# Loads of x gated, the first batch re-ordered, squares in pairs and second-layer work moved forward in a fused attention and feed-forward kernel

## Chip, cores and metric

The kernel runs on one core of one Trainium2 chip. The metric is the device time of one execution in microseconds (us). Executions of one kernel differ in time and in the clock that TensorE is granted, so several were taken of each. An execution more than 1.5% above the fastest of its kernel is labelled slow; on one core that is all a label can say.

TensorE is called PE, its weight load PEld, VectorE DVE, ScalarE ACT and GpSimd POOL. SP issues DMAs, and so does POOL. PSUM is the memory in which the kernel collects PE's sums. A transpose or load "lands" when its data is there.

## The reference, cut to what matters

```python
# x: 8 x 8 x 512 x 64, state: 8 x 8 x 32 x 64 (batch, head, tokens, depth), float32
scores = scale * x @ state.T ;  a  = softmax(scores)  ;  xread = a @ state
scores2 = scale * state @ x.T;  a2 = softmax(scores2) ;  sread = a2 @ x
X = concat([xread, sread], tokens)      # 544 tokens per batch, 512 features
r = maximum(X @ w_in, 0)                # w_in: 512 x 2048
out = (s * (r * r) + b) @ w_out         # w_out: 2048 x 512
```

## The kernel before

For each batch the kernel transposes x (`xT`), makes the scores `T`, their exponentials `E`, the sums `D`, the logarithm `L`, the reciprocal `R` and the weights `a`. It never forms `xread`: since `xread @ w_in` is `a @ (state @ w_in)`, it makes `M = state @ w_in` in four quarters and then `h = a @ M` in 16 tiles of 128 features. A tile is closed by a relu (`r`), a square (`g`) and later used by the second layer (`o`):

```python
    def mm1_close(key, hps, ntok, f):
        gt = gpool.tile([P, ntok], FP16, name=f"g_{key}_{f}", tag="g")
        r16 = rpool.tile([P, ntok], FP16, name=f"r_{key}_{f}", tag="r")
        if key == 0 and f % 4 == 1:
            nc.vector.tensor_scalar(r16, hps, 0.0, None, ALU.max)
        else:
            nc.scalar.activation(r16, hps, AF.Relu)
        nc.vector.tensor_mul(gt, r16, r16)
        G[key, f] = gt
```

The order of PE, SP and POOL is fixed by hand (`manual_schedule`). A "unit" is four second-layer matmuls; one follows each first-layer tile, and units lag about one batch behind. The batch `s` also prepares batch `s+1`:

```python
        for s in range(1, B):
            todo_s = pieces(s)
            for f in range(NKF):          # 16 tiles
                mm1_x(s, f)
                for fn in todo_s.get(f, []):
                    fn()
                if s == 1 and f == 4:
                    continue
                unit(todo.pop(0))
```

The loads of weights and of x, which also cast to 16 bits, go through one queue that POOL feeds: four quarters of `w_in` (wi), x1, `w_out` (wo), the state, x2 and then, at once, x3 to x7. From batch 2 on, `xT` is made by a DMA transpose that SP issues, as is `ET` (the transposed exponentials):

```python
            if s == 1:
                at(0, lambda: att_xT_dma(2))
                at(0, lambda: att_ET(0))
                at(0, lambda: att_ET(1))
                ...
                at(10, lambda: att_T(2, [0, 1]))
                at(11, lambda: att_ET(2))
                at(11, lambda: att_xT_dma(3))
```

Batch 0 is the opening: its x comes in float32 and is cast on DVE and ACT, and its transposes run on PE. A few idle matmuls (`warm_up`) keep PE active meanwhile.

The softmax here doesn't subtract the row's maximum and nothing guards it: scores larger than these inputs give would overflow.

## Time and profile before

| | before |
|---|---|
| median time (first runs) | 236.88 us (236.38 to 238.37, 3 runs) |
| profiled span | 235.9 us |
| PE busy | 220.0 us, 93% |
| first h of batch 1 starts | 32.46 us |
| PE ends | 232.6 us |

The profiled execution is not one of the three timed ones; it took 238.07 us at a mean granted clock of 0.971, among the slower of this kernel.

First, lines of the page of the kernel before: the busy time of PE, then the span in 40 slices of 5.9 us, where a digit is the busy share in tenths and 9 means 90% or more; PEclk is the granted clock in tenths of full speed.

```profile
...
PE 220.0 (93%) x1623; PEld 98.0 (42%) x1623; DVE 120.5 (51%) x269; ACT 122.4 (52%) x213; POOL 36.0 (15%) x67
...
PE   5989689989849999999999999999999999999994
...
PEclk9659999999988999999999999999999999999999
...
```

From about the fourteenth slice on PE is full, at full clock. What a change of order can win lies before 72 us. The next view lists what PE waited for: total us, how often, longest.

```profile
...
engine line waited for: us in total, times, longest us
PE T L64 <- DMA xT<-xn: 5.0, 2, 3.8
PE stTps L64 <- DVE st L461: 1.5, 1, 1.5
...
```

The largest is T, the scores of batches 2 and 3, waiting for the DMA transpose of x. The chain of waits of the kernel before, cut to 75 us, shows start, length, and what the time went to:

```profile
...
1.18 4.15 DMA stf<-in_state_dram
...
13.16 1.87 PE h L64 x4
...
19.13 0.68 DVE r L305
...
20.41 1.01 DVE g L308 x3
...
34.55 16.46 DMA xT<-xn
...
56.94 10.98 DMA xT<-xn
...
68.70 1.45 PE o L64 x4
...
```

The chain begins with the load of the state tile, runs through casts to the first h at 13.16, is mostly on DVE from 18.8 to 26.2 us, and then sits twice on a transpose: one issued at 34.55 that took 16.46 us to land, and one that took 10.98. The lines of SP in the timeline show why the second starts late: its issues stand in a fixed order, and the transpose of x3 stands behind the slow first one and three ET.

```profile
...
34.55 7.28 SPq L180 DMA_TRANSPOSE xT<-xn  x1
41.93 14.84 SPq L259 DMA_TRANSPOSE ET<-E  x3
56.94 5.61 SPq L180 DMA_TRANSPOSE xT<-xn  x1
```

Last, the busy time of each engine in chosen stretches of the kernel before (us, then per engine busy us and count; then granted clock, DMA share, GB/s):

```profile
...
core 0: us, PE busy (x) PEld busy (x) DVE busy (x) ACT busy (x) POOL busy (x), PEclk, DMA share, GB/s
4.20:7.60 3.40, 1.70 (x14) 0.67 (x12) 2.05 (x7) 1.15 (x3) 3.40 (x6) 1.00 1.19 285
7.60:17.85 10.25, 8.94 (x55) 3.05 (x56) 5.20 (x14) 6.46 (x15) 3.18 (x4) 0.50 1.30 204
20.00:25.00 5.00, 4.20 (x35) 2.00 (x34) 4.94 (x15) 2.84 (x6) 0.00 (x0) 1.00 1.24 206
65.60:69.00 3.40, 0.95 (x26) 0.51 (x27) 0.26 (x1) 0.42 (x1) 0.00 (x0) 1.00 0.52 151
69.00:72.40 3.40, 3.40 (x10) 1.18 (x8) 1.47 (x3) 1.44 (x5) 0.00 (x0) 0.51 0.00 0
...
```

Two stretches run at half clock, 7.6 to 17.85 and 69.0 to 72.4 us. Each follows a stretch of 3.4 us in which PE was busy half the time or less. The Trainium skill, "TensorE: Matmul & The Clock Gate", Part 1, puts PE at half rate after an idle window of about 3.4 us. From 20 to 25 us DVE is full.

### The profile page before, as it was taken

The page shows a single profiled execution, that of the slowest core. Times are in us where ns is not written, and L with a number is a line of the kernel's source. Part 1 is how long each engine was busy: PE and PEld are TensorE (multiplying, and loading weights), DVE is VectorE, ACT ScalarE, POOL GpSimd, SP SyncE. Part 2 cuts the span into 40 slices and gives each one's busy share as a digit, 9 for nine tenths or more (in the row PEclk, how much of TensorE's full clock was granted, in tenths as well). Part 3 has the DMA queues.
Part 4 walks back from the last instruction along what each step waited for, and adds up shares of the span by engine and source line. Part 5 has one row for each costly group of instructions (what it writes and reads, how often), then busy time and mean ns, then how long its engine had stood idle before and what let it go on. Part 6 is the DMA issues. An engine that isn't in the chain of part 4 may idle for free.

```text
span 235.9 us, 4108 instructions
## 1 busy us (share of the span) xinstructions
PE 220.0 (93%) x1623; PEld 98.0 (42%) x1623; DVE 120.5 (51%) x269; ACT 122.4 (52%) x213; POOL 36.0 (15%) x67
## 2 busy tenths in 40 slices
PE   5989689989849999999999999999999999999994
PEld 1323233334313444434443444344444444465653
DVE  1559844844523655474547454745474544533421
ACT  3566845358526634874487448744874444323300
POOL 8530053100100000000000000000000011000033
PEclk9659999999988999999999999999999999999999
DMA  6999999999930162621165116211311111111113
GB/s 192 210 202 207 202 126 136 146 183 221 169 121 0 47 152 74 148 74 47 44 148 78 44 49 150 74 47 44 89 47 44 44 47 46 65 72 44 44 44 89
DMA packets 38774, 23.68 MB, mean 100 GB/s; under 512 B 24100, under 2 KB 36644, under 8 KB 38756
## 3 DMA queue, kind: packets, MB, share of 16 engines
q0 software_dynamic: 15792, 16.72, 34.6%
q1 hardware_dynamic: 22548, 6.62, 17.6%
q8 instruction: 12, 0.20, 0.4%
q10 hardware_dynamic: 416, 0.10, 0.2%
q14 instruction: 6, 0.05, 0.1%
HBM read 17.33 MB, written 8.91 MB: 111 GB/s over the span
## 4 chain that ended last, share of the span: by engine, by line
PE 79%; DMA 13%; DVE 4%; ACT 2%; issue 1%; ACTq 0%
PE o L64 44%; PE h L64 20%; DMA xT<-xn 12%; PE Mps L64 3%; PE h_sr L64 3%; PE o_sr L64 3%; DMA stf<-in_state_dram 2%; PE D L64 2%; PE T L64 1%; PE V L64 1%; DVE g L308 1%; DVE M L249 1%; DVE xT L173 1%; PE xTps L64 1%; ACT r L307 1%
## 5 line engine op out<-in xcount | busy, mean ns | idle before, releaser
L64 PE MATMUL o<-wo,g 128*128 128x512 f16 (+1 forms) x528 | 132.4, 376 | 0.7 <-ACT M L250 0.7
L307 ACT ACTIVATE r<-h 128x512 f16<-128x512 f32 x124 | 73.5, 597 | 73.5 <-PE h L64 73.4
L308 DVE TENSOR_TENSOR g<-r 128x512 f16<-128x512 f16 x128 | 53.7, 423 | 63.0 <-ACT r L307 61.9
L64 PE MATMUL h<-a,M 128*128 128x512 f16 x256 | 77.6, 390 | 2.8 <-DVE M L249 1.4
L64 PEld LDWEIGHTS <-g 128*128 128x128 f16 x528 | 49.0, 98 | 55.5 <-issue 8.9
L350 POOL DMA_DIRECT2D out_dram<-osb x31 | 16.9, 544 | 166.9 <-DVE osb L348 128.0
L64 PEld LDWEIGHTS <-M 128*128 128x128 f16 x256 | 25.1, 100 | 35.0 <-issue 6.3
L348 DVE SCALAR_TENSOR_TENSOR osb<-o,s_bc,bias_bc 128x512 f32<-128x512 f32 (+1 forms) x33 | 24.1, 730 | 4.1 <-PE o L64 4.0
L254 DVE CAST M<-Mps 128x1024 f16<-128x1024 f32 x13 | 15.9, 1220 | 4.7 <-PE Mps L64 4.6
L64 PE MATMUL Mps<-wi,stT 64*32 64x512 f16 x256 | 13.5, 397 | 0.7 <-ACT r L307 0.4
L252 ACT CAST M<-Mps 128x1024 f16<-128x1024 f32 x13 | 13.1, 1008 | 0.0
L64 PEld LDWEIGHTS <-stT 64*32 64x32 f16 x384 | 4.7, 90 | 19.4 <-issue 15.4
L203 ACT ACTIVATE E<-T 128x512 f16<-128x512 f32 x16 | 9.4, 596 | 6.4 <-PE T L64 6.4
L307 ACT ACTIVATE r_sr<-h_sr 128x256 f16<-128x256 f32 x16 | 6.1, 384 | 11.4 <-PE h_sr L64 11.3
L228 DVE TENSOR_TENSOR a<-E,R 128x1024 f16<-128x1024 f16 (+1 forms) x9 | 5.7, 632 | 10.0 <-ACT R L227 10.0
L308 DVE TENSOR_TENSOR g_sr<-r_sr 128x256 f16<-128x256 f16 x16 | 4.7, 292 | 10.1 <-ACT r_sr L307 9.5
L64 PE MATMUL h_sr<-srdT,wi 128*128 128x256 f16 x64 | 9.3, 272 | 0.1
L64 PE MATMUL T<-xT,stT 64*32 64x256 f16 x128 | 4.0, 288 | 5.0 <-DMA xT<-xn 5.0
L227 ACT ACTIVATE R<-L 128x1024 f16<-128x1024 f32 (+1 forms) x9 | 8.5, 959 | 0.2
L226 ACT ACTIVATE L<-D 128x1024 f32<-128x1024 f32 (+1 forms) x9 | 8.3, 924 | 0.2 <-PE D L64 0.2
L64 PEld LDWEIGHTS <-wi 128*128 128x128 f16 x64 | 6.2, 97 | 3.7 <-issue 0.4
L64 PE MATMUL o_sr<-wo,g_sr 128*128 128x512 f16 x32 | 7.1, 379 | 0.0
(53 smaller groups left out, 90.1 us busy)
## 6 DMA issues: line engine op xcount, KB each, us to landing
out_dram<-osb POOLq DMA_DIRECT2D x31, 256.0 KB, 2.5
xn<-in_x_dram POOLq DMA_DIRECT2D x7, 512.0 KB, 15.3
wi<-in_moe_w_in_dram POOLq DMA_DIRECT2D x4, 512.0 KB, 10.5
wo<-in_moe_w_out_dram POOLq DMA_DIRECT2D x4, 512.0 KB, 19.7
xf<-in_x_dram SPq DMA_DIRECT2D x2, 512.0 KB, 5.0
out_dram<-osb_sr POOLq DMA_DIRECT2D x8, 64.0 KB, 1.9
out_dram<-osb SPq DMA_DIRECT2D x2, 128.0 KB
st<-in_state_dram POOLq DMA_DIRECT2D x1, 192.0 KB, 19.6
```

What stands on the lines that cost most here:

```text
L64: return nc.tensor.matmul(out, lhsT, rhs, start=start, stop=stop, tile_position=tp, is_transpose=is_transpose, skip_group_check=True,)
L173: eng(dst[:, h2 * i : h2 * i + h2], two[i].rearrange("p (q t) -> p q t", q=h2),)
L203: nc.scalar.activation(a["E"][:, g, :].rearrange("p (m t) -> p m t", m=2), T[:, :, 256 * i : 256 * i + 256], AF.Exp, scale=scale, accum_ou ...
L226: nc.scalar.activation(a["L"][:, sl], Dps, AF.Ln)
L227: nc.scalar.activation(a["R"][:, sl], a["L"][:, sl], AF.Exp, scale=-1.0)
L228: nc.vector.tensor_mul(a["a4"][:, sl], a["E"][:, sl], a["R"][:, sl])
L252: nc.scalar.copy(dst, ps)
L254: nc.vector.tensor_copy(dst, ps)
L307: nc.scalar.activation(r16, hps, AF.Relu)
L308: nc.vector.tensor_mul(gt, r16, r16)
L348: nc.vector.scalar_tensor_tensor(osb, ops, s_bc, bias_bc[:, n0:n1], ALU.mult, ALU.add)
L350: eng.dma_start(dst, osb[p0:p1])
```

## The change

Its intent: keep x loads away from the transposes that PE needs next; shorten the chain of the opening; save DVE time by squaring two tiles at once; and give PE second-layer work inside batch 0, where it has gaps. The diff is cut to its core; some smaller moves are left out (the PSUM pool of some h tiles, and the places of the bias sum and of two M copies in batch 1):

```diff
     def mm1_close(key, hps, ntok, f):
+        if f % 2 == 0:
+            R2[key] = rpool.tile([P, 2, ntok], FP16, ...)
+        r16 = R2[key]
+        if key == 0 and f in (1, 5):                 # was f % 4 == 1
+            nc.vector.tensor_scalar(r16[:, f % 2], hps, 0.0, None, ALU.max)
         ...
+        if f % 2 == 1:
+            nc.vector.tensor_mul(gt, r16, r16)       # 128 x 2 x ntok
@@ issue order on POOL
         load_wi(0)
         load_wi(1)
+        cast_st(nc.gpsimd, 0, 1)
         load_wi(2)
+        cast_x0(1, 1, nc.gpsimd.tensor_copy)
+        cast_st(nc.gpsimd, 1, 2)
         load_x(1)
         load_wi(3)
         ...
-        for b in range(3, B):
-            load_x(b)
@@ batch 0, start
-        warm_up(8); cast_st; att_stT(0); cast_x0 x4; att_xT_pe(0, 0); warm_up(2)
-        att_xT_pe(0, 1); att_T(0, [0]); warm_up(1); att_T(0, [1]); att_D(0, [0])
-        cast_st; att_stT(1); att_D(0, [1]); att_M(0, 0)
+        warm_up(11); cast_x0 x2; att_xT_pe(0, 0); att_stT(0); cast_x0; warm_up(2)
+        att_T(0, [0]); att_xT_pe(0, 1); att_D(0, [0]); warm_up(1); att_T(0, [1])
+        att_stT(1); att_M(0, 0); att_D(0, [1]); warm_up(2)
@@ batch 0, rest
-            7: [att_M(1, 0, "split")], 9: [broadcast_sb, att_xT_pe(1, 0)],
-            10: [att_xT_pe(1, 1)], 11: [att_M(0, 3, "split"), att_T(1)],
-            13: [att_D(1)], 14: [att_M(1, 1, "split")]
+            7: [att_xT_pe(1, 0)], 8: [broadcast_sb], 9: [att_xT_pe(1, 1)],
+            10: [att_M(0, 3, "dve"), att_T(1)], 11: [att_D(1)],
+            12: [att_M(1, 0, "act"), unit(units[0])], 13: [unit(units[1])],
+            14: [att_M(1, 1, "dve"), unit(units[2])], 15: [unit(units[3])]
-        for i in range(2): unit(units[i])            # two units after batch 0
@@ batches 1 and later
+            nc.gpsimd.tensor_copy(gate, A[2]["xT"][0:1, 0, 0, 0:1])   # POOL waits for xT of x2
+            load_x(3)
-                at(11, lambda: att_xT_dma(3))
+                at(8, lambda: att_xT_dma(3))
+                at(12, lambda: load_x(4))
+            if s + 3 < B: at(9, lambda: load_x(s + 3))
```

More of the change, by code (lines that the diff above doesn't have):

```diff
@@ L52 @@
     apool = ctx.enter_context(tc.tile_pool(name="apool", bufs=2))
-    gpool = ctx.enter_context(tc.tile_pool(name="gpool", bufs=3 * NKF))
+    gpool = ctx.enter_context(tc.tile_pool(name="gpool", bufs=3 * NKF // 2))
     rpool = ctx.enter_context(tc.tile_pool(name="rpool", bufs=4))
@@ L90 @@
     st16 = konst.tile([P, 2 * B, 2, D], FP16, name="st16")
+    gate = konst.tile([1, 1], FP16, name="gate")
     xf = konst.tile([P, NG, NQ, SCH * D], FP32, name="xf")
@@ L249, in att_M @@
             nc.vector.tensor_copy(dst[:, 0], two[0])
-            nc.scalar.copy(dst[:, 1], two[1])
+            (nc.vector.tensor_copy if b + c == 0 else nc.scalar.copy)(dst[:, 1], two[1])
         elif how == "act":
@@ L293 @@
     G = {}
+    R2 = {}
     def mm1_open(key, ntok, f):
@@ L297, in mm1_open @@
         if key == 0 and f % 2 == 1:
-            pool, tag = (psA, "att") if f < 8 else (psO, "o")
+            pool, tag = (psA, "att") if f < 8 else (psH, "h")
         return pool.tile([P, ntok], FP32, tag=tag, name=f"h_{key}_{f}")
     def mm1_close(key, hps, ntok, f):
-        gt = gpool.tile([P, ntok], FP16, name=f"g_{key}_{f}", tag="g")
-        r16 = rpool.tile([P, ntok], FP16, name=f"r_{key}_{f}", tag="r")
-        if key == 0 and f % 4 == 1:
-            nc.vector.tensor_scalar(r16, hps, 0.0, None, ALU.max)
-        else:
-            nc.scalar.activation(r16, hps, AF.Relu)
-        nc.vector.tensor_mul(gt, r16, r16)
-        G[key, f] = gt
+        if f % 2 == 0:
+            R2[key] = rpool.tile([P, 2, ntok], FP16, name=f"r_{key}_{f}", tag="r")
+        r16 = R2[key]
+        if key == 0 and f in (1, 5):
+            nc.vector.tensor_scalar(r16[:, f % 2], hps, 0.0, None, ALU.max)
+        else:
+            nc.scalar.activation(r16[:, f % 2], hps, AF.Relu)
+        if f % 2 == 1:
+            gt = gpool.tile([P, 2, ntok], FP16, name=f"g_{key}_{f}", tag="g")
+            nc.vector.tensor_mul(gt, r16, r16)
+            G[key, f - 1] = gt[:, 0]
+            G[key, f] = gt[:, 1]
     def mm1_k(b, f, g, hps):
@@ L459, in cast_st, with cast_x0 @@
         def cast_st(eng, b0, b1):
-            for k in range(2):
-                eng.tensor_copy(st16[:, 2 * b0 : 2 * b1, k, :], stf[:, 2 * b0 : 2 * b1])
+            n = 2 * (b1 - b0)
+            src = stf[:, 2 * b0 : 2 * b1].unsqueeze(2).broadcast_to([P, n, 2, D])
+            eng.tensor_copy(st16[:, 2 * b0 : 2 * b1], src)
+        def cast_x0(g, half, eng):
+            h2 = NQ // 2
+            src = xf[:, g, half * h2 : half * h2 + h2]
+            dst = xn[0].rearrange("p (q g) c d -> p g q (c d)", g=NG)[
+                :, g, half * h2 : half * h2 + h2
+            ]
+            eng(dst, src)
         load_wi(0)
         load_wi(1)
+        cast_st(nc.gpsimd, 0, 1)
         load_wi(2)
+        cast_x0(1, 1, nc.gpsimd.tensor_copy)
+        cast_st(nc.gpsimd, 1, 2)
         load_x(1)
@@ L472 @@
         nc.gpsimd.tensor_copy(st16[:, 4:, 1, :], st16[:, 4:, 0, :])
-        for b in range(3, B):
-            load_x(b)
-        def cast_x0(g, half, eng):
-            h2 = NQ // 2
-            src = xf[:, g, half * h2 : half * h2 + h2]
-            dst = xn[0].rearrange("p (q g) c d -> p g q (c d)", g=NG)[
-                :, g, half * h2 : half * h2 + h2
-            ]
-            eng(dst, src)
-        warm_up(8)
-        cast_st(nc.vector, 0, 1)
+        warm_up(11)
+        cast_x0(0, 0, nc.vector.tensor_copy)
+        cast_x0(0, 1, nc.scalar.copy)
+        att_xT_pe(0, 0)
         att_stT(0)
-        for g in range(NG):
-            cast_x0(g, 0, nc.vector.tensor_copy)
-            cast_x0(g, 1, nc.scalar.copy)
-        att_xT_pe(0, 0)
+        cast_x0(1, 0, nc.vector.tensor_copy)
         warm_up(2)
+        att_T(0, [0])
         att_xT_pe(0, 1)
-        att_T(0, [0])
+        att_D(0, [0])
         warm_up(1)
         att_T(0, [1])
-        att_D(0, [0])
-        cast_st(nc.vector, 1, 2)
         att_stT(1)
+        att_M(0, 0, "split")
         att_D(0, [1])
-        att_M(0, 0, "split")
+        warm_up(2)
         mm1_x4(0, 0, lambda: att_M(0, 1, "split"))
@@ L504 @@
             5: [lambda: att_M(0, 2, "split")],
-            7: [lambda: att_M(1, 0, "split")],
-            9: [broadcast_sb, lambda: att_xT_pe(1, 0)],
-            10: [lambda: att_xT_pe(1, 1)],
-            11: [lambda: att_M(0, 3, "split"), lambda: att_T(1, [0, 1])],
-            13: [lambda: att_D(1, [0, 1])],
-            14: [lambda: att_M(1, 1, "split")],
+            7: [lambda: att_xT_pe(1, 0)],
+            8: [broadcast_sb],
+            9: [lambda: att_xT_pe(1, 1)],
+            10: [lambda: att_M(0, 3, "dve"), lambda: att_T(1, [0, 1])],
+            11: [lambda: att_D(1, [0, 1])],
+            12: [lambda: att_M(1, 0, "act"), lambda: unit(units[0])],
+            13: [lambda: unit(units[1])],
+            14: [lambda: att_M(1, 1, "dve"), lambda: unit(units[2])],
+            15: [lambda: unit(units[3])],
         }
@@ L515, with gated_x3 @@
                 fn()
-        for i in range(2):
-            unit(units[i])
-        todo = units[2:]
+        todo = units[4:]
+        def gated_x3():
+            nc.gpsimd.tensor_copy(gate, A[2]["xT"][0:1, 0, 0, 0:1])
+            load_x(3)
         def pieces(s):
@@ L528, in pieces @@
                 at(0, lambda: att_xT_dma(2))
+                at(0, gated_x3)
                 at(0, lambda: att_ET(0))
                 at(0, lambda: att_ET(1))
-                at(1, lambda: att_M(1, 2, "dve"))
-                at(3, lambda: att_M(1, 3, "act"))
-                at(4, bias_sum)
-                at(5, bias_end)
+                at(8, lambda: att_xT_dma(3))
+                at(12, lambda: load_x(4))
+                at(3, lambda: att_M(1, 2, "dve"))
+                at(5, lambda: att_M(1, 3, "act"))
+                at(2, bias_sum)
+                at(3, bias_end)
                 at(6, lambda: att_stT(2))
@@ L544, in pieces @@
                 return out
+            if s + 3 < B:
+                at(9, lambda: load_x(s + 3))
             if nb < B:
@@ L570 @@
                     fn()
-                if s == 1 and f == 4:
+                if s == 1 and f == 2:
                     continue
```

## The prediction

> **What bounds the kernel now.** TensorE (PE). The page gives PE 220.0 of 235.9 us (93%), DVE 51%, ACT 52%. From 70 to 232.6 us the slices show PE without gaps. What can be won lies before 72 us:
>
> - Opening (0 to 32.5 us, where the first matmul of batch 1 starts). The chain of waits runs DMA of the state tile to 5.3, casts, transposes, exponentials, first h at 13.16; from 18.8 to 26.2 it sits on DVE (r, M casts, g, xT copies). DVE is busy 4.94 of the 5 us from 20. The granted clock is 0.50 from 7.6 to 17.85 us, after a stretch (4.2 to 7.6) in which PE was busy only 1.70 of 3.4 us.
> - Two waits for the DMA transposes of x: 1.14 us at 51 and 3.81 us at 68 (waits of PE). Those transposes took 16.5 and 11.0 us from issue to landing against 4.3 for the best one, because five x loads queued at 33 us share the engines. The 3.8 us gap also brings a half clock from 69.0 to 72.4, about 1.7 us more. The Trainium skill, "TensorE: Matmul & The Clock Gate", Part 1, gives half rate after one idle window of about 3.4 us; the trace agrees (0.5, in multiples of 3.41 us).
>
> **What the change does.**
>
> 1. Gating x3 behind xT2, spreading x4 to x7, and issuing xT3 three slots earlier. x2 lands near 34.4 as before; xT2 then runs nearly alone (landed near 40, needed near 45); xT3 lands near 52, needed near 59. Gain: 1.1 + 3.8 + 1.7 = 6.6 us, all on the critical path.
> 2. Opening order. The x0 cast no longer waits behind the state casts on DVE; E0 starts near 7.6 instead of 9.25, first h near 11.9 instead of 13.2, the second half of h near 13.2 instead of 15.5. Extra warm-ups (5 matmuls) fill otherwise idle PE and probably keep the clock. GpSimd casts delay the issue of later loads by about 3 us, but the software queue is serial at about 2.6 us per 0.5 MB tensor and has issues in hand: no later landings.
> 3. Squares in pairs: 128x512 took 423 ns, 128x1024 (a<-E,R) 692, so 154 ns per pair, about 1.2 us of DVE in batch 0; two relu's (0.69 us each) go from DVE to ACT. Later DVE is half idle: worth nothing.
> 4. Four second-layer units (0.86 us each) sit inside batch 0 in idle PE, against two after it. Batch 1 starts near 30.0 instead of 32.5 with 1.73 us more work done: opening gain about 4.2 us.
>
> **Prediction.** 236.9 - 6.6 - 4.2 + about 0.3 for clock risk: **226.3 us**, 8 in 10 within 223.5 to 229.5. Faster by over 2%: 0.95; within 2%: 0.04; slower: 0.01.
>
> **What would show it.** Waits of PE on DMA xT gone; granted clock 1.0 at 65 to 75; batch 1's first h near 30; first second-layer matmul near 25 instead of 30.7; g in 64 plus 8 pairs of about 0.69 us and 0.42 us.
>
> **What would make it wrong.** PE near 20 to 24 us waits for DVE, then ACT's exponentials: a window under half busy would bring a half clock there (1 to 2 us). The half clock at 7.6 may remain. GpSimd casts slower than 1 us would delay wi2, x1 and everything behind them, x2 and xT2 included. The GpSimd gate holds back the first outputs; if that reached the output buffers, DVE and then PE would stall.

## The result, and the profile after

| | before | after |
|---|---|---|
| median time | 237.41 us (236.38 to 238.37, 4 runs) | 225.44 us (225.28 to 225.51, 4 runs) |
| profiled span | 235.9 | 223.5 |
| PE busy | 220.0 (93%) | 215.9 (97%) |
| first h of batch 1 | 32.46 | 28.95, with two more units done |
| PE ends | 232.6 | 220.1 |

The ratio is 0.9495 (95% interval 0.945 to 0.9541). Ratios here are the mean time of one kernel's fast runs over that of the other's of the same rounds, so not quite the ratio of the medians quoted. PE starts the first h of batch 1 earlier, before and after:

```profile
...
32.46 0.59 PE L64 MATMUL h<-a,M 128*128 128x512 f16 x2
...
28.95 0.59 PE L64 MATMUL h<-a,M 128*128 128x512 f16 x2
...
```

The page of the changed kernel, the same lines (slices of 5.6 us):

```profile
...
PE 215.9 (97%) x1628; PEld 97.8 (44%) x1628; DVE 113.2 (51%) x191; ACT 121.9 (55%) x211; POOL 37.7 (17%) x71
...
PE   7887999999999999999999999999999999999993
...
PEclk9999999999999999999999999999999999999999
...
```

PE is at 90% or more from the fifth slice to the last but one, and the clock is never lowered. The waits of PE in the changed kernel:

```profile
...
PE warm_ps L64 <- DVE warm L447: 1.2, 1, 1.2
PE Mps L64 <- DMA wi<-in_moe_w_in_dram: 0.9, 1, 0.9
PE D L64 <- DVE M L255: 0.5, 1, 0.5
PE xTps L64 <- DMA xn<-in_x_dram: 0.5, 1, 0.5
...
```

No wait for a transpose is left; two small waits for loads (wi, x1) are new. SP's lines in the timeline:

```profile
...
34.55 1.98 SPq L181 DMA_TRANSPOSE xT<-xn  x1
36.64 3.06 SPq L260 DMA_TRANSPOSE ET<-E  x2
46.22 2.85 SPq L181 DMA_TRANSPOSE xT<-xn  x1
...
```

The transpose of x2 is issued at 34.55 as before, but occupies SP for 1.98 us instead of 7.28, and the one of x3 goes out at 46.22 instead of 56.94. The stretches, for comparison:

```profile
...
4.20:7.60 3.40, 3.22 (x25) 1.41 (x24) 1.70 (x4) 1.33 (x3) 1.93 (x4) 1.00 1.19 279
7.60:17.85 10.25, 8.96 (x74) 3.52 (x74) 8.02 (x16) 7.72 (x16) 6.68 (x9) 1.00 1.30 206
20.00:25.00 5.00, 3.99 (x44) 1.43 (x45) 2.85 (x6) 3.90 (x9) 0.00 (x0) 1.00 1.24 206
...
```

The bookkeeping of the profiled spans: 235.9 - 223.5 = 12.4 us. Up to the first h of batch 1 the gain is 32.46 - 28.95 = 3.5 us, and two units more are done by then (8 matmuls at 0.216 us, 1.7 us): 5.2 us. The other 7.2 us are the two waits (1.14 + 3.81), about 1.8 us of half clock behind the second (the four o matmuls at 68.70 took 1.45 us on the chain of waits and the next four 1.65, against 0.86 at full clock; the h between them 0.85 against 0.43), and 0.35 us before the bias matmul.

This compares a longer than usual execution of the kernel before (238.07 us, clock 0.971, half clock for 10.24 us of its opening) with an ordinary one of the changed kernel (225.28 us). Profiles of the same old opening in other runs reached the first h of batch 1 sooner: at 30.86 us with no half clock (fill_wait) and at 31.07 and 31.90 us with 3.4 us of it (gate_warm, which has three more idle matmuls, and gate_only). So about 1.6 of the 5.2 us go with the clock of that one execution.

### The profile page after: what moved, and what is told of

It is laid out like the page before. It is cut to its first block, busy times and chain, and to the rows that moved or that the text cites. A ratio compares the mean times of both kernels' runs of the same rounds, so it can differ in the third digit from the quotient of the medians.

```text
span 223.5 us, 3970 instructions
## 1 busy us (share of the span) xinstructions
PE 215.9 (97%) x1628; PEld 97.8 (44%) x1628; DVE 113.2 (51%) x191; ACT 121.9 (55%) x211; POOL 37.7 (17%) x71
## 4 chain that ended last, share of the span: by engine, by line
PE 89%; DMA 8%; DVE 1%; POOL 1%; SPq 0%; issue 0%
PE o L64 51%; PE h L64 22%; DMA wi<-in_moe_w_in_dram 5%; PE Mps L64 4%; PE h_sr L64 3%; PE o_sr L64 3%; DMA stf<-in_state_dram 2%; PE D L64 2%; PE V L64 1%; PE T L64 1%; DVE M L255 1%; PE bias_ps L64 0%; PE wsum_ps L64 0%; SPq L450 0%; POOL xn L106 0%; PE stTps L64 0%
## 5 line engine op out<-in xcount | busy, mean ns | idle before, releaser
L310 ACT ACTIVATE r<-h 128x512 f16<-128x512 f32 x126 | 74.3, 597 | 70.3 <-PE h L64 66.5
L64 PE MATMUL h<-a,M 128*128 128x512 f16 x256 | 75.5, 379 | 0.3 <-ACT r L310 0.3
L313 DVE TENSOR_TENSOR g<-r 128x1024 f16<-128x1024 f16 x64 | 44.1, 691 | 44.0 <-ACT r L310 43.6
L356 POOL DMA_DIRECT2D out_dram<-osb x31 | 16.9, 546 | 147.1 <-DVE osb L354 136.2
L64 PEld LDWEIGHTS <-M 128*128 128x128 f16 x256 | 24.6, 98 | 30.2 <-issue 1.7
L255 DVE CAST M<-Mps 128x1024 f16<-128x1024 f32 x15 | 18.3, 1223 | 2.5 <-PE Mps L64 2.2
L253 ACT CAST M<-Mps 128x1024 f16<-128x1024 f32 x14 | 14.1, 1008 | 0.0
L64 PE MATMUL Mps<-wi,stT 64*32 64x512 f16 x256 | 12.6, 383 | 1.0 <-DMA wi<-in_moe_w_in_dram 0.9
L64 PE MATMUL warm_ps<-warm 128*128 128x512 f16 x16 | 6.4, 549 | 1.3 <-DVE warm L447 1.2
L313 DVE TENSOR_TENSOR g_sr<-r_sr 128x512 f16<-128x512 f16 x8 | 3.4, 426 | 6.6 <-ACT r_sr L310 6.3
```

The source lines that it names most:

```text
L64: return nc.tensor.matmul(out, lhsT, rhs, start=start, stop=stop, tile_position=tp, is_transpose=is_transpose, skip_group_check=True,)
L253: nc.scalar.copy(dst, ps)
L255: nc.vector.tensor_copy(dst, ps)
L310: nc.scalar.activation(r16[:, f % 2], hps, AF.Relu)
L356: eng.dma_start(dst, osb[p0:p1])
```

## The experiments

Every experiment passed the check of its result. That includes no_load_wait, which computes the wrong thing, so on these inputs the check does not see that error. All were timed in five rounds against the kernel before. On those chips the kernel before took 237.13 to 237.79 us (medians of 11 runs). The changed kernel, repeated as a yardstick, took 225.65. It was repeated on one chip only, beside gate_only, no_gate and fill_wait; the other runs are compared with it across chips, on which the fast mean of the kernel before ranges from 236.2 to 237.4 us. Differences of under 1 us between such runs are soft.

**after_again: the changed kernel once more** (no edit).

> The changed kernel unchanged, as the yardstick on this chip. 225.3 to 225.6 us, ratio to before 0.945 to 0.954.

Measured: 225.65 us (225.32 to 227.02), ratio 0.9519 (0.9476 to 0.9563). The median is 0.05 above the range expected; the ratio is as expected. An effect below about 0.4 us is not told apart here.

### What the gate is worth

**gate_only: the gate without the rest.** In the kernel before:

```diff
-        for b in range(3, B): load_x(b)
+            gate copy, load_x(3) after xT of x2; load_x(4) at tile 12; load_x(s + 3) at tile 9
-                at(11, lambda: att_xT_dma(3))
+                at(8, lambda: att_xT_dma(3))
```

> The kernel before with only the gating of the x loads (x3 after the transpose of x2, x4 to x7 spread over the batches, transpose of x3 three slots earlier). My theory: the two waits of PE for the transposes (1.1 and 3.8 us) and the half clock after the second (1.7 us) go, so about 6.6 us faster than before, near 230.5 us; the opening keeps its 32.5 us and its half clock from 7.6 to 17.9. Rival A: the transposes are slow by themselves, or because of the stores and the other transposes, not because of the x loads: then the transpose of x3 still takes 10 us or more and the gain is under 3 us. Rival B: the gain needs the new opening as well: under 3 us.

Measured: 230.14 us (228.04 to 231.87), ratio 0.9667. On fast runs that is 7.5 us less than the kernel before (229.43 against 236.93); the medians differ by 7.4. PE's waits for transposes are gone from its profile. SP's lines:

```profile
...
34.60 1.98 SPq L181 DMA_TRANSPOSE xT<-xn  x1
...
46.99 6.35 SPq L181 DMA_TRANSPOSE xT<-xn  x1
...
```

Both rivals fall: the two transposes landed after 6.3 and 8.4 us instead of 16.5 and 11.0, and the gain needs no new opening. In this run the load of x4 (45.4 to 53.4 us) ran beside the second.

**no_gate: the rest without the gate.** In the changed kernel the loads of x3 to x7 go back behind x2, and the transpose of x3 to tile 11.

> The changed kernel with the loads of x put back as before (all five behind x2, transpose of x3 in its old place). My theory: the waits come back in full, since the new opening makes PE need the transposes earlier while x2 still lands at 34.4 us: 6.5 to 9 us slower than the changed kernel, 232 to 234 us, with PE waiting for the transposes of x2 and x3[...]. Rival (terms do not add): the opening and the gate share their gain, so that without the gate the opening's 5 us are lost again in the wait for x3, which is set by the DMA queue and not by PE: then near 236 us, equal to before within 1 us.

Measured: 235.77 us (234.21 to 238.98), ratio 0.9919 (0.9868 to 0.9969); on fast runs 9.5 us slower than the changed kernel and only 1.5 us faster than the kernel before. My range was 6.5 to 9, so the rival is nearer. Its PE waits hold this line:

```profile
...
PE T L64 <- DMA xT<-xn: 7.3, 2, 4.0
...
```

PE waited 7.3 us instead of 5.0. T of batch 3 starts at 66.74 us against 68.05 in the kernel before, though its first h of batch 1 started at 29.29 instead of 32.46: the transposes, not PE, set that time. So the terms do not add. The gate alone gives 7.5 us, the rest alone 1.5, both together 11.0 (236.93 - 225.92, same chip). Most of the opening's gain only counts once the gate has taken the transposes off the chain. The two waits also speak to the clock:

```profile
...
49.51 0.44 PE L64 MATMUL T<-xT,stT 64*32 64x256 f16 x16 [3.27 <-DMA xT<-xn]
49.88 1.04 PE L64 MATMUL o<-wo,g 128*128 128x512 f16 x4
...
66.74 0.65 PE L64 MATMUL T<-xT,stT 64*32 64x256 f16 x16 [4.05 <-DMA xT<-xn]
...
67.75 1.89 PE L64 MATMUL o<-wo,g 128*128 128x512 f16 x4
...
```

After a wait of 3.27 us four o matmuls took 1.04 us, full clock; after one of 4.05 us they took 1.89.

**fill_wait: does the half clock cost extra?** In the kernel before:

```diff
+                if s == 2:
+                    at(3, lambda: warm_up(9))
                 at(3, lambda: att_T(nb, [0, 1]))
```

> The kernel before with nine idle matmuls (1.9 us) put on PE inside its 3.8 us wait for the transpose of x3; they do nothing but keep PE active. My theory: the half clock from 69 to 72.4 us follows from the idle window and costs 1.7 us beyond the wait itself, so this kernel is 1.3 to 1.9 us faster than before though it does more work, and the clock stays at 1.0 at 65 to 75 us. Rival: the half clock costs nothing, or comes from something else: same time within 0.5 us.

Measured: 235.92 us (235.38 to 237.29), ratio 0.9955 (0.9905 to 1.0005). Medians differ by 1.65 us, fast means by 0.8, and the interval touches 1: the sign is likely, the size not settled. The profile shows why: the half clock after the second wait is gone, but in this execution the first wait, 2.0 us long, brought one. Its stretches:

```profile
...
48.40:51.81 3.41, 1.50 (x21) 0.69 (x22) 1.54 (x2) 1.17 (x4) 0.00 (x0) 0.96 1.35 183
51.81:55.22 3.41, 3.41 (x10) 1.19 (x9) 0.59 (x2) 0.95 (x4) 0.00 (x0) 0.54 1.36 184
...
```

PE was busy 1.50 of 3.41 us, and the next stretch ran at about half clock. (The trace's own clock record puts the change at 51.57 us; in the 3.42 us before it PE was busy for 1.42.)

A second reading of the clock needs no edit. The kernel before was executed 44 times beside the experiments, and 31 of these count as fast. Among the fast ones the eight with a mean granted clock of 0.99 or more took 235.9 us on average, the 17 between 0.98 and 0.99 took 237.0, and the six below 0.98 took 237.4. The changed kernel's ten executions all had 0.997 or more. So a part of the gain, of the order of 1 us, goes along with the clock; this is a correlation and not a test.

### What the opening is made of

**single_sq: one square per tile.** In the changed kernel:

```diff
-        if f % 2 == 1: nc.vector.tensor_mul(gt, r16, r16)
+        nc.vector.tensor_mul(gt[:, f % 2], r16[:, f % 2], r16[:, f % 2])
```

> The changed kernel with one square per tile of 128x512 again instead of one per pair. The prediction took 1.2 us of DVE time off a chain that it called DVE bound: then this is 1.0 to 1.4 us slower, near 226.8. My theory after seeing the trace: in the changed kernel PE waits in batch 0 for the loads of x1 and the last quarter of w_in (0.5 and 0.9 us), not for DVE, and a pair has to wait for both of its halves, so the pairing is worth nothing: within 0.4 us of 225.5.

Measured: 225.6 us (225.36 to 225.99), ratio 0.95. The pairing is worth nothing that can be seen. DVE was busy 7.74 of the 8 us from 13 to 21 us with single squares and 7.08 with pairs: 0.66 us saved, and spent waiting.

**fewer_warm: without the five added idle matmuls** (`warm_up(11)` to `warm_up(8)`, `warm_up(2)` ahead of the first h removed).

> The changed kernel without the five added idle matmuls (8 instead of 11 at the start, none ahead of the first h). Theory: they are what keeps the clock at 1.0 in the opening; without them a window with under half of it busy lets the clock fall to 0.5 between 7 and 18 us in most executions: 0.5 to 2 us slower, mean clock 0.98 to 0.995, larger spread. Rival: the new order alone keeps PE busy enough: within 0.3 us of 225.5, clock 1.0.

Measured: 225.5 us (225.29 to 225.67), mean clock 0.99 to 1.0. The rival holds: the added idle matmuls are worth nothing that can be seen.

**units_after: no units inside batch 0.**

```diff
-            12: [..., unit(units[0])], 13: [unit(units[1])], 14: [..., unit(units[2])], 15: [unit(units[3])]
+        for i in range(2): unit(units[i])      # after batch 0; todo = units[2:]
```

> The changed kernel with no second-layer unit inside batch 0; two follow it, as before the change. Theory: PE has no work to do while the exponentials of batch 1 are made (the first h of batch 1 can't start before 26.5 us), so of the 3.5 us of units about 1 us can't be hidden elsewhere: 0.7 to 1.5 us slower, near 226.6. Rival: batch 1 simply starts earlier by as much: within 0.3 us.

Measured: 227.58 us (227.11 to 229.08), ratio 0.9596; on fast means 2.0 to 2.5 us slower than the changed kernel. That is more than expected. In its PE timeline (start, us, operation, idle time before it) the gap is plain:

```profile
...
25.64 0.41 PE L64 MATMUL Mps<-wi,stT 64*32 64x512 f16 x8
27.46 0.59 PE L64 MATMUL h<-a,M 128*128 128x512 f16 x2 [1.42 <-ACT r L310]
...
```

The last h of batch 0 has to wait 1.42 us for the relu of an earlier tile to free its PSUM buffer, while ACT makes the reciprocal and copies M for batch 1 (1.06 and 1.01 us, from 24.95 on). In the changed kernel the units run there.

**casts_off_pool: casts on DVE and ACT, loads issued without a break.**

```diff
-        cast_st(nc.gpsimd, 0, 1) ... cast_x0(1, 1, nc.gpsimd.tensor_copy); cast_st(nc.gpsimd, 1, 2)
+        cast_st(nc.vector, 0, 1) ... cast_x0(1, 1, nc.scalar.copy); cast_st(nc.vector, 1, 2)
```

> The changed kernel with the casts of the state and of the last quarter of x0 on DVE and ACT instead of GpSimd, so that all loads are issued without a break. Theory: the loads land when the serial queue lets them, not when they are issued, so x1 and the last quarter of w_in land as before (16.7 and 19.3 us), and the exponentials start about 0.5 us later, which the waits for those loads swallow: 0 to 0.5 us slower. Rival A: the GpSimd casts delay the loads: 0.5 us or more faster, x1 landing earlier. Rival B: the cast chain is critical: 0.7 us or more slower.

Measured: 225.65 us (225.56 to 226.63). This matters for reading the chain of waits of the changed kernel:

```profile
...
7.42 0.40 POOL st L468
7.82 0.83 POOL xn L106
8.65 11.73 DMA wi<-in_moe_w_in_dram
...
20.52 0.45 PE Mps L64 x8
...
21.00 1.24 DVE M L255
...
```

Read naively, it says that the cast of the state on POOL (7.42) held up the issue of x1 (7.82), so that the last wi was issued at 8.65 and PE got it at 20.4. In casts_off_pool POOL issues the same loads at 4.23 and 5.10:

```profile
...
4.23 0.92 POOL L106 DMA_DIRECT2D xn<-in_x_dram  x1
5.10 0.80 POOL L112 DMA_DIRECT2D wi<-in_moe_w_in_dram  x1
...
```

They land at 16.9 (x1) and 20.6 us (wi), against 16.8 and 20.4 in the changed kernel (the expectation says 16.7 and 19.3; the record of landings has these). Issued 3.5 us earlier, they land no sooner: in the changed kernel the first four loads of this queue land at 9.0, 11.6, 14.1 and 16.8 us, one about every 2.6 us, and the wait belongs to the bytes ahead, not to the issue.

**no_load_wait: the two load waits taken away.** Wrong: batch 0 multiplies with the third quarter of `w_in` in place of the fourth, and the transposes of batch 1 read x0.

```diff
-   xn[b][...]                          # in att_xT_pe
+   xn[0][...]
-   wi[c][...]                          # in att_M
+   wi[min(c, 2) if b == 0 else c][...]
```

> Wrong result on purpose. The changed kernel, where batch 0 uses the third quarter of w_in in place of the fourth and the transposes of batch 1 read x0 in place of x1, so that the two waits of PE for loads in the opening (0.5 to 0.9 us for x1, 0.9 us for w_in) have no cause; all loads still run. Theory: the changed kernel's opening is bound by these two loads: 1.0 to 1.8 us faster than it, 223.7 to 224.5. Rival: DVE and the exponentials bind it all the same: within 0.4 us of 225.5.

Measured: 225.25 us (224.59 to 226.2). That is 0.4 us under the yardstick's median and 0.2 under that of the first runs, where 1.0 or more was expected. My theory, that the loads alone bind the new opening, falls. With the load waits gone, its profile has these instead:

```profile
...
PE D L64 <- ACT E L204: 0.9, 3, 0.4
PE T L64 <- DVE xT L174: 0.9, 1, 0.9
...
```

T of batch 1 now waits for DVE's copies of xT and starts at 20.60, against 20.82 us. Loads, DVE and the exponentials end within a few tenths of each other, so removing one alone gains next to nothing. That fits the null result of single_sq too. It is read from the trace; no run removed two of them at once.

**swap_loads: a proposal.** The last quarter of `w_in` is loaded ahead of x1, and batch 0's last M moves to tile 7; the transposes of x1 move to tiles 11 and 12, the scores to 13, the sums to 14.

> A proposal. The changed kernel with the last quarter of w_in loaded ahead of x1, and batch 0's remaining first-layer tiles computed while x1 is under way; the transposes of x1, the exponentials of batch 1 and the same four units follow later. Theory (the loads bind the opening, in the order they are needed): h of batch 1 starts near 27.5 instead of 28.95 us, so 0.8 to 1.6 us faster than the changed kernel, near 224.3. Rival: the chain x1, transposes, exponentials, a of batch 1 becomes the bound as it starts 2.5 us later: same time or slower.

Measured: 226.16 us (225.95 to 227.26), ratio 0.9565, so no better and by the medians 0.5 us worse. The rival holds: T of batch 1 starts at 23.77 us instead of 20.82, ACT's logarithm and reciprocal follow late, and behind them ACT's copy of M, for which the first h of batch 1 waits 0.7 us; it starts at 29.68. No version tried beats the changed kernel by more than the noise.

**gate_warm: is the old opening's clock lost at its first gap?** gate_only with `warm_up(11)` in place of `warm_up(8)`.

> The kernel before with the gating of the x loads, as in gate_only, and 11 instead of 8 idle matmuls at the start, so that PE's gap ahead of the first transposes is filled. In gate_only the executions whose mean clock was 1.0 took 228.0 to 229.6 us, those at 0.991 to 0.997 took 230.7 to 231.9. Theory: the half clock in the opening is worth about 1.7 us and comes from that gap: median 228.5 to 229.2 us, mean clock 0.999 or more in all executions, smaller spread. Rival: the clock is lost elsewhere in the old opening (it has further waits of PE up to 30 us): same median as gate_only, 229.5 to 231, clock still below 1.0 in half of the executions.

Measured: 229.8 us (228.89 to 230.47), clock 1.0 in only one of six executions. The rival holds. PE's line at the first h of its timeline:

```profile
...
12.08 1.86 PE L64 MATMUL h<-a,M 128*128 128x512 f16 x4 [1.32 <-DVE a L229]
...
```

PE waited 1.32 us here, and four matmuls took 1.86 us; the clock record has half clock from 11.83 us. Filling the first gap did not save the clock; the gap ahead of the first h is in the old order itself.

**old_start: the old start in the changed kernel**, up to the first h (order, 8 idle matmuls, no POOL casts).

> The changed kernel with the chain of batch 0 up to its first h put back as it was before (order, 8 idle matmuls, no GpSimd casts); the gating, the pairs and the units inside batch 0 stay. The prediction credited the new order with the first h 1.3 us and its second half 2.3 us earlier, and with the clock. Theory: the old order brings back PE's wait of 1.1 to 1.3 us ahead of the first h and with it a half clock for 3.4 to 7 us, the first h near 12 to 13 instead of 11.4 us; of the delay the waits for x1 and w_in swallow some, and 1.0 to 2.5 us are left: 226.5 to 228, with a clock below 1.0 in most executions. Rival: loads and DVE bind batch 0 so far that the start is worth nothing: within 0.5 us of 225.5.

Measured: 226.78 us (226.18 to 228.32), ratio 0.9615; 1.05 us slower by fast means (226.97 against 225.92), 1.1 to 1.3 by medians, across chips. The mean clock was below 1.0 in five of six executions, though not in the profiled one:

```profile
...
12.09 1.02 PE L64 MATMUL h<-a,M 128*128 128x512 f16 x4 [1.32 <-DVE a L229]
...
```

The wait of 1.32 us is back; the first h starts 0.67 us later (12.09 against 11.42). This execution kept its clock and its span is only 0.5 us above the changed kernel's. The five others had a mean clock of 0.977 to 0.992 and were not profiled.

## Why the prediction was right

The prediction was 226.3 us, and 225.44 was measured. The mechanism was right where most of the gain lies, in the gate; of the rest, some credits were misplaced. That the sum still came out within 0.9 us is in part luck.

1. **The gate (predicted 6.6 us, all critical): right.** gate_only measured 7.5 us on fast runs. The transposes kept the predicted timetable: that of x2 landed at 38.9 us (predicted 40) and was needed at 45.7 (45), that of x3 landed at 52.6 (52) and was needed at 58.8 (59). The Trainium skill, "DMA: Bandwidth & Descriptors", section "SWDGE vs HWDGE vs iDMA", says that the software and the hardware queues feed different queues of each DMA engine, and that the engine takes them in turn. The traces agree that the two kinds slow each other: with five x loads queued the first transpose took 16.5 us, and ahead of them about 4.4. That they take turns is not shown by itself.
2. **Adding the terms: right only in this order.** The prediction summed gate and opening. With the gate in place the opening's term is 3.5 us by fast means and 4.5 by medians (gate_only against after_again); without it, 1.5 us are left of it (no_gate), since the transposes land when the DMA queue lets them.
3. **The opening (predicted 4.2 us, measured 3.5 to 4.5 with the gate in place): right in sum, wrongly divided.** The 5.2 us of the spans hold about 1.6 us of an unlucky clock. The units inside batch 0 are worth about 2 us (units_after) and the new start about 1.1 (old_start). The step "Squares in pairs", said to take 1.2 us of DVE off the opening, was worth nothing (single_sq): the durations were right (692 ns predicted and 691 measured for a pair), but 0.66 us came free only to be spent waiting. Any rest, from the other moves inside batch 0, was not tried by itself.
4. **The clock: right in effect, wrong in cause.** The prediction gave the extra idle matmuls credit ("probably keep the clock"). fewer_warm shows that they are not needed, and old_start, where a mean clock below 1.0 is back in five of six executions, that the new start keeps it. As neither the idle matmuls (fewer_warm) nor the POOL casts (casts_off_pool, clock 1.0 in all six) are needed for that, the order is what is left; the two were not taken away together. The feared half clock at 20 to 24 us did not come: PE was busy 3.99 of the 5 us from 20.
5. **"No later landings" in spite of the POOL casts: right** (casts_off_pool).

The prediction was 0.9 us too high. The gate alone came out 0.9 us larger than predicted, and the 0.3 us set aside for the clock were not needed; how the rest divides is within the spread of the kernel before (its fast executions on one chip took 235.35 to 238.54 us).

What stays open: the exact price of one half-clock window; how much of the gain over the kernel before is its clock; and whether the earlier issue of the transpose of x3 adds to the gate, which were only tried together.

## What to carry to other kernels

When two transfers share the DMA engines, hold back the one that is not needed yet; look for it where a transfer takes several times its best time from issue to landing. Before adding up gains, ask which event fixes the end of each stretch: an earlier start is worth little in front of a wait that something else times. And when several chains end at nearly the same moment, shortening one of them shows in its own busy time and not in the kernel's.

## What the Trainium skill lacked or had wrong

- "TensorE: Matmul & The Clock Gate", section "Why this matters for your kernels", advises no PE-idle gaps above about 3 us. These runs do not follow the length of a gap: one of 2.0 us was followed by half clock in fill_wait, one of 3.27 us in no_gate was not. They follow better how long PE was busy in the window of 3.41 us before, for which the page has no figure. Windows with 1.00 and 1.71 us (before), 1.14 (no_gate) and 1.42 (fill_wait) were followed by half clock; the gap of 3.27 us fell across two windows with 1.75 and 1.81 us, and the clock stayed. It is no sharp limit: 1.77 us (gate_only) and 1.95 (gate_warm) were followed by half clock too, 1.82 (old_start) was not. No window at full clock in which PE was busy for 2.0 us or more was followed by half clock in these traces. PE's busy time is modelled, so such small differences say little.
- "DMA: Bandwidth & Descriptors" has no figure for a DMA transpose that runs beside casting loads: 16.5 and 11.0 us from issue to landing in the kernel before, against 4.4 to 6.3 us in the changed kernel.
